# Loading the second chunk of two weight matrices in halves, and multiplying it half by half for two batches together

## The chip, the cores and the metric

The kernel runs on one core of one Trainium2 chip. The core has a matmul engine (PE, with its weight loads shown apart as PEld), a vector engine (DVE), an activation engine (ACT), a general engine (POOL) and a queue engine (SP), and 16 DMA engines that move data between the chip's main memory (DRAM) and the on-chip memory. The metric is the device time of one execution in microseconds; smaller is better.

## What is computed

The inputs are q, k and v of 8 batches x 8 heads x 576 positions x 64, a memory score phi of 8 x 8 x 576 x 32, and three weight matrices: gate and value (512 x 1536) and out (1536 x 512). Cut to what matters:

```python
a = softmax(phi, over the 576 positions)
k_m = einsum('bhsm,bhsd->bhmd', a, k)        # 32 memory slots per head
v_m = einsum('bhsm,bhsd->bhmd', a, v)
attn = softmax(scale * q @ k_m.T)            # 576 x 32 per head
x = attn @ v_m                               # (batch, 576, 512) over all heads
out = (silu(x @ w_gate) * (x @ w_val)) @ w_out
```

## The kernel before, in words

The kernel never forms x. For each batch it multiplies the small v_m (32 slots x 64 per head) by the gate and value weights first. The result is called U here: 8 heads x 32 slots = 256 rows by 1536 columns, once for gate and once for value. Then gate = attn @ U_gate and value = attn @ U_value. The 1536 columns are cut into three chunks of 512 (`CH`), and each chunk can be cut into two halves of 256 (`HC`).

**Loads of the weights.** `load_w(which, c, half)` (issue at L155) loads chunk `c` of the gate weights (`which` 0) or the value weights (`which` 1), from float32 in DRAM to bfloat16 on the chip. Without `half` it is one load of 512 KB with 512 columns in a row; with `half` it is one load of 256 KB with 256 columns in a row. The tile of a chunk in halves has the half as its outer dimension, and `w_part` (L158 to L164) picks the right slice for either layout. Before the change chunk 0 is loaded in halves (four loads of 256 KB) and chunks 1 and 2 whole (four loads of 512 KB).

**The POOL queue.** POOL issues all these loads, and also those of k, v, q, most of phi and the out weights, and it does arithmetic between them: in the opening it multiplies one attention tile (`norm(1, 1, nc.gpsimd)`, L512), and later it forms sums of activations (L637, L680). Its instructions run in the order written. The loads that POOL issues share eight semaphores in rotation, so that each load is issued only after the load eight places earlier has landed. The order of POOL's loads before is: k of batch 0, q of batch 0, k of batch 1, q of batch 1, v of batches 0 and 1, chunk 0 in four halves, chunk 1 (gate, value), chunk 2 (gate, value); then the multiplication L512; then out weights 0, k of batch 2, out weights 1, phi of batch 2, out weights 2, v of batch 2; then, between groups of sums, phi of batch 3, q of batch 2, q of batch 3, k and v of batch 3. In this text "q of batch 2" is the load issued at L125 at 42.64 us.

**The weight products.** `u_round` (L520 to L576) multiplies one or more parts of the weights by v_m of one batch. A part is one or two of gate and value, a chunk, and one or both halves. The 128 x 128 array of PE is used as eight tiles of 64 x 32, so eight matmuls (L531) run side by side. Each part fills two PSUM banks of 512 columns, which are then copied to the U tile by ACT (L560) and DVE (L564), in the order of the letters in `evac`. `u_item(b, c)` is one round with all of chunk c of gate and then of value: 16 matmuls of 512 columns and four copies of 512 columns. `u_half(b, (0, 1), c, half, evac)` is one round with one half of gate and of value side by side: 16 matmuls of 256 columns and two copies of 512 columns.

**The slots.** A slot (`gv_slot`, L622) is 128 of the 1536 columns for half the positions of one batch: two matmuls of 288 columns for the gate (p_g, L592), a silu on ACT (L609), and one slot later two matmuls for the value (p_v, L592) and a product on DVE (L615). A batch has 24 slots, eight to a chunk. `g0` and `g1` are the slots of batches 0 and 1. When the eight slots of a chunk are through, `chunk_done` (L663) hands sums over the chunk to POOL or DVE and issues some later loads.

**The order around the change.** Batches 0 and 1 run together. Everything is written out by hand (`manual_schedule`), so the order of the program is the order on each engine. Chunk 0 already runs in halves for both batches. Then, before the change, the loop over chunks 1 and 2 does: products of batch 0, some slots of batch 1's previous chunk, five slots of batch 0; products of batch 1, three slots of batch 0, five slots of batch 1. From batch 2 on, each batch needs its q transposed: `q_T` (L432 to L442) does that for batch 2 on PE with q as the loaded weights (p_q, L438), amid output products of batch 0 (L814) and the k and v sums of batch 2 (p_kv, L248).

Of the kernel before, what the change touches and what calls it, by code (L numbers as in the profile page):

```python
# [14 lines left out]
def kernel(  # L15
# [34 lines left out]
    NCH = DF // CH  # L50
# [46 lines left out]
    def load_k(b):  # L97
        t = inp.tile(
            [128, 2 * NP + (b % 2 == 0), JK * D], BF16, tag=f"kv{b % 2}", bufs=1, name="t_kv"
        )  # L100
        nc.gpsimd.dma_start(out=t[:, 0:NP], in_=head_pairs(k[b]))  # L101
        kvs[b] = t

    def load_v(b):
        t = kvs[b]
        if b in counted:
            out = t[:, NP + 1:2 * NP + 1][:, ::-1]
        else:
            out = t[:, NP:2 * NP]
        nc.gpsimd.dma_start(out=out, in_=head_pairs(v[b]))  # L110
# [32 lines left out]
    HC = CH // 2  # L143

    def load_w(which, c, half=None):

        src = (moe_w_gate, moe_w_val)[which]
        split = half is not None
        if not half:
            W[which, c] = wpool.tile(  # L150
                [128, 2, NP, HC] if split else [128, NP, CH], BF16,
                tag=f"W{which}{c}", name=f"W{which}{c}",
            )
        f0, n = (half * HC, HC) if split else (0, CH)
        nc.gpsimd.dma_start(  # L155
            out=W[which, c][:, half] if split else W[which, c],
            in_=src[:, c * CH + f0:c * CH + f0 + n].rearrange("(i p) f -> p i f", p=128),
        )  # L158

    def w_part(which, c, i, g, halves):  # L160

        w = W[which, c][64 * g:64 * g + 64]
        h0, h1 = halves[0], halves[-1] + 1
        return w[:, h0:h1, i] if c == 0 else w[:, i, HC * h0:HC * h1]  # L164

    WO, WOc, Ts = {}, {}, {}

    def load_wo(c):
        t = wpool.tile([128, 4, DM], BF16, tag=f"WO{c}", name=f"WO{c}")
        nc.gpsimd.dma_start(  # L170
            out=t,
            in_=moe_w_out[c * CH:(c + 1) * CH, :].rearrange("(i p) f -> p i f", p=128),
        )
        for i in range(4):
            WO[4 * c + i] = t[:, i]
        WOc[c] = t
# [333 lines left out]
    def norm(b, g, eng=nc.vector):  # L510
        a = att.tile([128, 2, HALF], BF16, tag=f"A{g}", name="t_A")
        eng.tensor_tensor(out=a, in0=es.pop((b, g)), in1=lzs.pop((b, g)), op=ALU.mult)  # L512
        atts[b, g] = a
# [6 lines left out]
    def u_round(b, parts, evac, later=None, sums=None):  # L520
# [3 lines left out]
        for which, c, halves in parts:  # L524
# [4 lines left out]
            def one(w, i, g, p=p, n=n, w0=w0, c=c, halves=halves):  # L529
                o = (w - w0) * n  # L530
                nc.tensor.matmul(  # L531
                    p[g][32 * i:32 * i + 32, o:o + n],
                    lhsT=kTs[b][64 * g:64 * g + 64, 2, 32 * i:32 * i + 32],
                    rhs=w_part(w, c, i, g, halves),
                    start=True,
                    stop=True,
                    tile_position=(64 * g, 32 * i),
                )
# [43 lines left out]
    def flush_mul(n=None):  # L582
        for _ in range(len(pend) if n is None else n):
            pend.pop(0)()
# [349 lines left out]
    def u_item(b, c, evac="avav"):  # L934

        return lambda: u_round(b, (((0,), c, (0, 1)), ((1,), c, (0, 1))), evac)

    def u_half(b, which, c, half, evac):

        return lambda: u_round(b, ((which, c, (half,)),), evac)  # L940
# [18 lines left out]
    def run(items):  # L959
        for x in items:  # L960
            x()
# [13 lines left out]
    def gv_slots(b):  # L975
        return [lambda s=s: gv_slot(b, s) for s in range(2 * NJF)]
# [36 lines left out]
    load_q(1)  # L1013
    load_v(0)
    load_v(1)
    for half in range(2):
        for which in range(2):
            load_w(which, 0, half)
    for c in range(1, NCH):
        for which in range(2):  # L1020
            load_w(which, c)
    for c in range(NCH):
        u_buffer(1, c, f"S{c}")

# [25 lines left out]
    z_inv(1, 1)  # L1050
    norm(1, 0)
    norm(1, 1, nc.gpsimd)
    load_wo(0)
    load_k(2)
    nc.gpsimd.memset(kvs[2][:, NP], 1.0)
# [9 lines left out]
    g0, g1 = gv_slots(0), gv_slots(1)  # L1065
# [15 lines left out]
    run(last_copy)  # L1081
    flush_mul(1)
    run(g1[2:4] + g0[4:8] + g1[4:6])
    for c in range(1, NCH):
        s = 8 * c
        run([u_item(0, c)] + g1[s - (2 if c == 1 else 3):s] + g0[s:s + 5])
        run([u_item(1, c)] + g0[s + 5:s + 8] + g1[s:s + 5])
    run(g1[-3:])
    flush_mul()
    backlog = []  # L1090

# [158 lines left out]
```

## Time and profile before

| | |
|---|---|
| median of 3 runs | 231.17 us (231.09 to 231.43) |
| profiled execution, its own time | 231.35 us |
| span of that execution | 229.6 us |
| PE busy | 221.1 us (96%) |
| DVE busy | 186.6 us (81%) |
| ACT busy | 171.2 us (75%) |
| POOL busy | 151.8 us (66%) |
| mean share of DMA queue q0 (POOL's loads) | 52.9% |

The span runs from the first to the last instruction; the device time has some 1.75 us around it. Times inside the profile are counted from the start of the span. A busy PE is not PE at its peak, since matmuls are pipelined, so the stretch around the change is read from the timeline and the chain of waits and not from the busy share. In a line of the timeline the columns are: start, length, engine, line of the program, operation, what is written and read with its shape, and how many instructions are merged; in brackets stands how long the engine had been idle and for what.

### The profile page before, as it was taken

To read this page: it belongs to the slowest core of one execution; us is meant where nothing else is said; L and a number is where in the kernel's file an instruction comes from. 1 tells how busy PE (TensorE), PEld (TensorE's weight loads), DVE (VectorE), ACT (ScalarE), POOL (GpSimd) and SP (SyncE) were. 2 spreads that over 40 slices of the span, in tenths; PEclk is the share of its full clock that TensorE was granted. 3 is DMA by queue.
4 is the path that set the end of the run, shared out by engine and by line. 5 is a ranking of instruction groups with operands and counts; after the bars stand their busy time and mean duration, and the time that the engine had idled before them with its cause. 6 is when DMAs were issued, how large, how long until landed. Compare 5 with 4: busy or idle time off the path is not lost.

```text
span 229.6 us, 7220 instructions
## 1 busy us (share of the span) xinstructions
PE 221.1 (96%) x2826; PEld 171.3 (75%) x2826; DVE 186.6 (81%) x425; ACT 171.2 (75%) x365; POOL 151.8 (66%) x207
## 2 busy tenths in 40 slices
PE   6986899999999999999999999999999999999993
PEld 2553576778887877888788887888788878878893
DVE  4156799999977999998997768998999899977832
ACT  2867988988446899988885758978898889677311
POOL 8422736999099759979986789467545764029291
PEclk9999999999999999999999999999999999999998
DMA  6999999999995998998199945995013502202024
GB/s 207 213 211 205 198 207 207 211 256 267 207 175 135 236 276 168 223 201 205 62 227 197 204 149 120 252 226 100 32 62 113 107 0 96 91 0 94 23 92 163
DMA packets 36546, 36.84 MB, mean 160 GB/s; under 512 B 14496, under 2 KB 30880, under 8 KB 36512
## 3 DMA queue, kind: packets, MB, share of 16 engines
q0 software_dynamic: 16272, 22.42, 52.9%
q1 hardware_dynamic: 19568, 13.24, 21.6%
q10 hardware_dynamic: 672, 0.72, 0.9%
q8 instruction: 22, 0.36, 0.6%
q14 instruction: 12, 0.10, 0.1%
HBM read 42.47 MB, written 9.44 MB: 226 GB/s over the span
## 4 chain that ended last, share of the span: by engine, by line
PE 87%; DMA 9%; POOL 2%; issue 0%; ACT 0%; POOLq 0%; ACTq 0%
PE p_g L592 21%; PE p_v L592 21%; PE p_os L814 20%; PE p_oc L814 10%; DMA W<-in_moe_w_val_dram 9%; PE p_oa L814 5%; PE p_u L531 5%; PE p_kv L248 2%; PE p_os L802 1%; PE p_g L451 1%; POOL t_kv L101 1%; POOL t_kv L110 1%; POOL t_q L125 0%; PE p_q L438 0%; POOL W L155 0%
## 5 line engine op out<-in xcount | busy, mean ns | idle before, releaser
L615 DVE TENSOR_TENSOR t_h<-t_sg,p_v 128x288 bf16<-128x288 bf16 x192 | 82.1, 451 | 12.5 <-PE p_v L592 6.6
L592 PEld LDWEIGHTS <-t_U 128*128 128x128 bf16 x768 | 74.0, 98 | 20.2 <-issue 2.7
L609 ACT ACTIVATE t_sg<-p_g 128x288 bf16<-128x288 f32 x192 | 74.3, 420 | 17.8 <-PE p_g L592 11.1
L592 PE MATMUL p_g<-t_A,t_U 128*128 128x288 bf16 x384 | 77.0, 286 | 0.0
L592 PE MATMUL p_v<-t_A,t_U 128*128 128x288 bf16 x384 | 77.0, 286 | 0.0
L814 PEld LDWEIGHTS <-t_S 128*128 128x128 bf16 x384 | 37.3, 98 | 4.6 <-issue 0.2
L680 POOL TENSOR_TENSOR t_S<-t_h 128x512 bf16<-128x512 bf16 x17 | 19.6, 1154 | 21.0 <-DVE t_h L615 19.7
L814 PEld LDWEIGHTS <-t_h 128*128 128x128 bf16 x288 | 27.0, 98 | 7.3 <-issue 3.5
L558 ACT CAST t_U<-p_u 128x512 bf16<-128x512 f32 x50 | 26.4, 608 | 4.8 <-PE p_u L531 4.8
L814 PE MATMUL p_os<-t_T,t_S 128*128 128x256 bf16 x192 | 23.7, 273 | 0.0
L637 POOL TENSOR_TENSOR t_S<-t_S,t_h 128x512 bf16<-128x512 bf16 x17 | 19.6, 1155 | 1.3
L637 POOL TENSOR_TENSOR t_S<-t_h 128x512 bf16<-128x512 bf16 x16 | 18.4, 1152 | 0.0
L637 POOL TENSOR_TENSOR t_S<-t_h,t_S 128x512 bf16<-128x512 bf16 x16 | 18.4, 1151 | 0.0
L531 PE MATMUL p_u<-W,t_kT 64*32 64x512 bf16 (+1 forms) x416 | 16.8, 363 | 0.5 <-DMA W<-in_moe_w_val_dram 0.4
L562 DVE CAST t_U<-p_u 128x512 bf16<-128x512 f32 x22 | 14.3, 684 | 1.5 <-PE p_u L531 1.4
L986 PE MATMUL p_warm<-bones 128*128 128x512 bf16 x44 | 13.2, 439 | 1.7 <-DVE bones L1008 1.7
L814 PE MATMUL p_os<-t_T,t_h 128*128 128x256 bf16 x96 | 14.8, 274 | 0.0
L392 ACT COPY t_q<-p_os 128x512 f32<-128x512 f32 (+2 forms) x12 | 5.5, 469 | 9.2 <-PE p_os L802 5.1
L814 PE MATMUL p_oc<-t_T,t_S 128*128 128x256 bf16 x96 | 12.1, 273 | 0.0
L814 PE MATMUL p_oa<-WO,t_h 128*128 128x256 bf16 x96 | 11.8, 273 | 0.0
L814 PE MATMUL p_oc<-WO,t_S 128*128 128x256 bf16 x96 | 11.8, 273 | 0.0
L814 PE MATMUL p_os<-WO,t_h 128*128 128x256 bf16 x96 | 11.8, 273 | 0.0
(115 smaller groups left out, 329.6 us busy)
## 6 DMA issues: line engine op xcount, KB each, us to landing
out_dram<-t_o SPq DMA_DIRECT2D x11, 512.0 KB, 3.1
t_kv<-in_k_dram POOLq DMA_DIRECT2D x8, 576.0 KB, 10.6
t_q<-in_q_dram POOLq DMA_DIRECT2D x8, 576.0 KB, 8.3
t_kv<-in_v_dram POOLq DMA_DIRECT2D x8, 576.0 KB, 15.6
t_phi<-in_phi_dram POOLq DMA_DIRECT2D x6, 576.0 KB, 8.2
out_dram<-t_o SPq DMA_DIRECT2D x10, 256.0 KB, 8.0
WO<-in_moe_w_out_dram POOLq DMA_DIRECT2D x3, 512.0 KB, 19.0
W<-in_moe_w_gate_dram POOLq DMA_DIRECT2D x2, 512.0 KB, 16.1
```

The lines of the kernel that those rows point to most:

```text
L248: nc.tensor.matmul(p[g][32 * i:32 * i + 32, 0:n], lhsT=phi_of(b, g, j, i), rhs=kv_of(b, slice(64 * g, 64 * g + 64), w0, w1, i, j), start=( ...
L392: nc.scalar.copy(out=out, in_=in_)
L531: nc.tensor.matmul(p[g][32 * i:32 * i + 32, o:o + n], lhsT=kTs[b][64 * g:64 * g + 64, 2, 32 * i:32 * i + 32], rhs=w_part(w, c, i, g, halve ...
L558: nc.scalar.copy(out=t, in_=p)
L562: nc.vector.tensor_copy(out=t, in_=p)
L592: nc.tensor.matmul(p[:, 0:HALF], lhsT=Us[b, c, g][:, o // 2, which, 128 * (o % 2):128 * (o % 2 + 1)], rhs=atts[b, g][:, r], start=(g == 0) ...
L609: nc.scalar.activation(out=sg, in_=gate[:, 0:HALF], func=AF.Silu)
L615: nc.vector.tensor_tensor(out=dst, in0=sg, in1=val[:, 0:HALF], op=ALU.mult)
L637: eng.tensor_tensor(out=out, in0=x, in1=y, op=ALU.subtract)
L680: eng.tensor_tensor(out=t[:, 0], in0=A21, in1=A22, op=ALU.add)
L814: nc.tensor.matmul(mine[home][:, u], lhsT=lhs(c, m, u), rhs=rhs(c, m), start=fresh and u == 0, stop=(k == 5), skip_group_check=u == 1 or n ...
L986: nc.tensor.matmul(p[:, 0:128 * a], lhsT=bones, rhs=x.to_broadcast([128, a, 128]) if a > 1 else bones, start=True, stop=True,)
```

## The change

The second chunk of the gate and value weights (c = 1) is loaded in four halves of 256 KB, in the order gate half 0, value half 0, gate half 1, value half 1, in place of two loads of 512 KB. The two loads of chunk 2 are issued later in POOL's program: behind the multiplication `norm(1, 1, nc.gpsimd)` and ahead of the out weights, so that still 14 loads stand ahead of that multiplication. The products of chunk 1 go by half chunks: half 0 for batch 0 and batch 1 one after the other, seven slots, half 1 for both, eight slots. The slots of the two batches are put in an order that fits: those of batch 0's chunk 1 come in two groups of four, and one slot of batch 1 follows each. Chunk 2 runs as before. In all later batches the matmuls with chunk 1 read the new layout of its tile.

```diff
@@ w_part
-        return w[:, h0:h1, i] if c == 0 else w[:, i, HC * h0:HC * h1]
+        return w[:, h0:h1, i] if c < 2 else w[:, i, HC * h0:HC * h1]
@@ the loads of the opening
-    for half in range(2):
-        for which in range(2):
-            load_w(which, 0, half)
-    for c in range(1, NCH):
-        for which in range(2):
-            load_w(which, c)
+    for c in range(2):
+        for half in range(2):
+            for which in range(2):
+                load_w(which, c, half)
@@ behind the attention of batch 1
     norm(1, 1, nc.gpsimd)
+    for which in range(2):
+        load_w(which, 2)
     load_wo(0)
     load_k(2)
@@ the slots of batches 0 and 1
     run(g1[2:4] + g0[4:8] + g1[4:6])
-    for c in range(1, NCH):
-        s = 8 * c
-        run([u_item(0, c)] + g1[s - (2 if c == 1 else 3):s] + g0[s:s + 5])
-        run([u_item(1, c)] + g0[s + 5:s + 8] + g1[s:s + 5])
-    run(g1[-3:])
+    for half, slots in enumerate((g1[6:8] + g0[8:12] + g1[8:9], g1[9:12] + g0[12:16] + g1[12:13])):
+        run([u_half(b, (0, 1), 1, half, "av") for b in range(2)] + slots)
+    run([u_item(0, 2)] + g1[13:16] + g0[16:21])
+    run([u_item(1, 2)] + g0[21:] + g1[16:])
     flush_mul()
```

## The prediction

> **What bounds the kernel now.** I read first the page's busy shares and the shares of the chain that ended last, then that chain in order of time, and then the timelines of PE and POOL where the change lies.
>
> ```profile
> PE 221.1 (96%) x2826; PEld 171.3 (75%) x2826; DVE 186.6 (81%) x425; ACT 171.2 (75%) x365; POOL 151.8 (66%) x207
> ...
> PE 87%; DMA 9%; POOL 2%; issue 0%; ACT 0%; POOLq 0%; ACTq 0%
> ```
>
> PE carries the end, after an opening that belongs to the DMA. The chain, in order of time (start, length, what):
>
> ```profile
> 6.74 20.12 DMA W<-in_moe_w_val_dram
> ...
> 34.71 0.56 PE p_u L531 x16
> ...
> 38.80 0.56 PE p_u L531 x16
> ```
>
> The value half 0 of chunk 0 lands at 6.74 + 20.12 = 26.86 us, last of the eight loads that PE needs to begin. Behind it the chain holds nothing but PE until the end of the kernel. PE's table of waits from 27 us to the end holds only the 0.4 us that this load ends, so a gain must come out of PE's own work and a loss must be a new PE wait. PE's timeline around a round in halves (chunk 0, today) and a whole round (chunk 1, today):
>
> ```profile
> 29.47 0.41 PE L592 MATMUL p_v<-t_A,t_U 128*128 128x288 bf16 x2
> 29.80 0.63 PE L531 MATMUL p_u<-W,t_kT 64*32 64x256 bf16 x32
> 30.37 0.66 PE L592 MATMUL p_v<-t_A,t_U 128*128 128x288 bf16 x4
> ...
> 34.30 0.41 PE L592 MATMUL p_v<-t_A,t_U 128*128 128x288 bf16 x2
> 34.64 0.62 PE L531 MATMUL p_u<-W,t_kT 64*32 64x512 bf16 x16
> 35.20 0.42 PE L592 MATMUL p_g<-t_A,t_U 128*128 128x288 bf16 x2
> ```
>
> From the last pair of a slot to the first of the next slot it is 30.37 - 29.47 = 0.90 us with 32 matmuls of 256 columns, and 35.20 - 34.30 = 0.90 us with 16 of 512.
>
> POOL's timeline shows when loads land, since each load waits for the one eight places earlier:
>
> ```profile
> 24.49 0.74 POOL L155 DMA_DIRECT2D W<-in_moe_w_val_dram  x1 [2.09 <-DMA t_kv<-in_v_dram]
> 25.27 1.29 POOL L512 TENSOR_TENSOR t_A<-t_E,t_lz 128x576 bf16<-128x576 bf16 x1
> 26.50 0.80 POOL L170 DMA_DIRECT2D WO<-in_moe_w_out_dram  x1
> ...
> 29.83 0.75 POOL L94 DMA_DIRECT2D t_phi<-in_phi_dram  x1 [0.43 <-DMA W<-in_moe_w_val_dram]
> 32.34 0.74 POOL L170 DMA_DIRECT2D WO<-in_moe_w_out_dram  x1 [1.76 <-DMA W<-in_moe_w_gate_dram]
> 34.90 0.74 POOL L110 DMA_DIRECT2D t_kv<-in_v_dram  x1 [1.81 <-DVE t_h L615]
> ```
>
> At 24.49 us v of batch 1 has landed, at 29.83 the four halves of chunk 0 behind it, at 34.90 the two whole loads of chunk 1 (the last line names DVE, but its load is the one eight behind the value weights of chunk 1). The stage table over those stretches (POOL busy, clock, DMA share, GB/s):
>
> ```profile
> 24.49:29.83 5.34, 4.77 (x6) 1.00 1.38 199
> 29.83:34.90 5.07, 1.49 (x2) 1.00 1.24 207
> ```
>
> The same megabyte takes 5.34 us in four halves and 5.07 us in two wholes. Last, the load of q of batch 2 and its user:
>
> ```profile
> 42.64 0.55 POOL L125 DMA_DIRECT2D t_q<-in_q_dram  x1
> ```
> ```profile
> DMA to landing us min/median/max: 16.7/16.7/16.7
> ```
> ```profile
> 58.99 0.61 PE L814 MATMUL p_oc<-t_T,t_S 128*128 128x256 bf16 x4
> 59.35 0.75 PEld L438 LDWEIGHTS <-t_q 128*128 128x128 bf16 x12
> 59.44 0.83 PE L438 MATMUL p_q<-ident,t_q 128*128 128x128 bf16 x12
> ```
>
> This load lands at 42.64 + 16.7 = 59.3 us and PE loads it as weights at 59.35. It comes just in time. It lies in one unbroken stream of loads: the DMA share is over 1 in every stretch of 2 us from 18 to 66 us.
>
> **The change part by part.**
>
> *Products of chunk 1.* Removed: two whole rounds at 34.64 and 38.73 us. Added: two pairs of half rounds, each 32 matmuls of 256 columns and 32 weight loads. By the rows above a pair costs 0.90 us against 0.90 us, so 0.00 us; I keep 0.02 as an upper bound, since the rows round to 0.01. The slots are the same in number: 7 + 8 before, 7 + 8 after, and the order from batch 1's slot 13 on is the old one.
>
> *Copies to U.* Four per round, two on ACT and two on DVE, before and after, of 512 columns each: 1.26 us for two on ACT and 1.40 us for two on DVE (35.11 and 35.19 us today). The first use comes two slots, 0.98 us, after the round, as now. DVE ends its second copy near 36.6 us, and PE wants that bank for the fourth pair after it, at 35.20 + 0.98 + 0.74 = 36.92. The 0.3 us between are the cover; ACT's first copy can start 0.05 us later (it needs 0.52 us after 29.80 in halves, 0.47 after 34.64 whole). Cost zero.
>
> *Later reads of chunk 1.* From batch 2 on its 512 columns are read as two runs of 256, as chunk 0 is now. A round of 24 matmuls, 16 on chunk 0 and 8 on chunk 1, takes 0.77 us in the chain, 32 ns a matmul, against 0.56 / 16 = 35 ns for chunk 1 alone. Bound 0 on both sides.
>
> *chunk_done.* Batch 0's chunk 1 finishes four slots (4 x 0.49 = 2.0 us) later, near 43.5 us. Its sums wait on POOL for their turn at 48.76 us, 5 us of cover, and for batch 1's slot 15, which does not move. Loads of k and v of batch 3 stand behind those sums and keep their place.
>
> *POOL.* Two more issues at 0.74 us. Fourteen loads still precede the multiplication L512, which waits for ACT, so it stays at 25.27; gate and value of chunk 2, moved from 21.66 and 24.49, go out at 26.50 and 27.3. With the rotation the others slip: the out weights to about 28.5, k of batch 2 to 29.83, the rest one landing each, v of batch 2 to 34.90 + 0.27 = 35.17. POOL is free at 35.9, before its first sum at 36.93. Since two loads were added, each load from phi of batch 3 on waits for the same load as now. SP's queue keeps its instructions; its first transposed load there needs q of batch 3, 0.3 us later with cover, since PE's scores with that q (L451) begin at 91.6 us.
>
> *DMA.* This is the one term that I find. No load changes its turn by bytes, and the stream stays full, since up to eight loads are in flight (15 to 20 us from issue to landing). But chunk 1 takes four transfers for two. Price: the rows 5.34 against 5.07 us give +0.27 us, 0.135 per added transfer. Bounds: by rate, 207 against 199 GB/s, 5.07 x 0.04 = +0.20; by the dearest pair of halves (26.86 to a landing of 12.49 + 17.1 = 29.6, so 2.73 us) 2 x 2.73 - 5.07 = +0.39. I take 0.27, which holds all four. What it delays: chunk 1's halves have cover (half 0 of both would land near 32.2 for 34.64; half 1 near 34.9 for 38.73), chunk 2 lands at 24.49 + 15.3 + 0.27 = 40.1 for 43.31. Out weights 0, k, phi and v of batch 2 have more than a microsecond each (v: 34.90 + 19.5 = 54.4 for 58.12). But q of batch 2 lands at 59.57 for a weight load at 59.35, where landing and load are 0 to 0.05 us apart today. PE then waits 0.22 to 0.27 us at p_q. All of batch 2, and the rest of PE's chain, stand behind it, and nothing there takes the time back.
>
> [...]
>
> Sum: 0.01 (products) + 0.25 (q of batch 2) = +0.26 us. The profiled execution's 231.35 becomes 231.61. It lies 0.18 above the median of the runs, so on the median's scale 231.17 + 0.26 = 231.43. A difference under 0.2%, 0.46 us, is about what a measurement can't tell from none, so this counts as no change with a lean to slower.
>
> **Rivals.**
>
> (a) The delay is hidden: in executions without a profile the loads may be a little earlier against PE. The profiled one is 0.18 us over the median, which would fit an opening, up to 26.86, slowed that much; then q of batch 2 has about 0.2 us of slack and costs 0.05. Or halves cost no more than wholes. Time 231.17 + 0.01 to 0.06, about 231.2. For it: the zero slack is a coincidence. Against: PE's start and this landing hang on the same stream, so both move together.
>
> (b) Slower by over 0.2%: the added transfers cost more than chunk 0's rows tell. Place: the same wait at p_q. It decides from 0.46 / 2 = 0.23 us per added transfer; the dearest pair of halves gives 0.195. At twice my price, 0.27, PE waits 0.54 and the time is 231.17 + 0.55 = 231.7. For it: loads of k and v of batch 2 and of phi share the stream until 59 us and my price is from one stretch. Against: four halves in a row already gave it.
>
> (c) Faster by over 0.2%: today the value weights of chunk 1 land at 18.77 + 15.8 = 34.6 us for matmuls that begin at 34.64; in runs where PE waits there, the change frees it, since half 0 is there 2.4 us ahead. It would have to remove over 0.46 us: 230.6. Against: the profiled execution waits 0.0 there, and a stream that is late at 34.6 is late at 59.3 too, where the change adds.
>
> (d) The change does what it says to order and loads; that PE itself runs differently (a bank or U not ready) I count into (b)'s side.
>
> **How the numbers follow.** Forecast (+0.1 to +0.45, own range 231.25 to 231.6): 0.48. Rival (a): 0.21. Rival (b), with (d): 0.24. Rival (c): 0.07. So faster 0.07, within 0.2% 0.48 + 0.21 = 0.69, slower 0.24. The time is the forecast's, 231.43. The range takes in (a) with 0.1 us of scatter below (the runs reach 0.08 under their median), 231.1, and (b) at twice the price with the same above, 231.8.
>
> **What would show it.** Right: POOL's load of v of batch 2 released near 35.2 in place of 34.90; chunk 1's rounds at 34.64 and near 38.7 with 32 matmuls in 0.56 us; PE idle some 0.25 us before p_q near 59.6 by the load of q; everything later shifted by that. Wrong: no idle time at p_q (rival a), over 0.45 us (b), or any new idle time of PE between 34 and 54 us (copies or banks late).

## The result and the profile after

The changed kernel took 232.05 us in the median of 20 runs (231.27 to 232.71). In the same session the kernel before took 231.11 us in the median of 20 runs (231.0 to 231.6). The ratio is 1.0038, with a 95% interval of 1.0027 to 1.0049: slower by about 0.9 us. The runs of the changed kernel also lie in a band twice as wide, 1.4 us against 0.6 us.

The profiled execution took 232.71 us with a span of 230.9 us, the slowest of those runs, 0.66 us above their median. The sum below is made against the profiled execution of before (231.35 us), so it has +1.36 us to explain, more than the medians differ.

Page of the changed kernel: busy shares, the row of the instruction queue (transfers, MB, share of 16 engines' span), and shares of the chain that ended last.

```profile
PE 220.2 (95%) x2858; PEld 171.1 (74%) x2858; DVE 186.7 (81%) x425; ACT 171.4 (74%) x365; POOL 153.4 (66%) x209
...
q8 instruction: 22, 0.36, 0.6%
...
PE 83%; DMA 10%; POOL 3%; ACT 1%; issue 1%; DVE 1%; POOLq 0%; ACTq 0%
```

PE was busy for 0.9 us less than before and yet ended later, so it stood idle. It runs 2858 matmuls and 2858 weight loads, 32 of each more than before. Its table of waits from 27 us to the end (us in total, times, longest) has two rows:

```profile
PE p_os L814 <- POOL t_S L637: 1.1, 1, 1.1
PE p_u L531 <- DMA t_kT<-t_bkv: 0.2, 1, 0.2
```

Neither is where the change lies. Where each of them falls is seen when the same instruction is timed in both kernels. After minus before is -0.20 us from 26.7 to 110 us, since this execution's opening happened to end 0.20 us sooner (first value half landed at 26.66 us against 26.86). It is +0.11 from 110.6 us on, and +1.41 from 134.1 us on (1.36 at the end). So there are two losses, 0.31 us and 1.30 us, and both are more than 65 us behind the changed part. PE's timeline of the changed kernel at the larger one:

```profile
132.30 0.41 PE L592 MATMUL p_g<-t_A,t_U 128*128 128x288 bf16 x2
132.54 0.41 PE L592 MATMUL p_v<-t_A,t_U 128*128 128x288 bf16 x2
134.10 0.60 PE L814 MATMUL p_os<-t_T,t_Q 128*128 128x256 bf16 x4 [1.14 <-POOL t_S L637]
```

The same place before:

```profile
132.44 0.41 PE L592 MATMUL p_v<-t_A,t_U 128*128 128x288 bf16 x2
132.69 0.60 PE L814 MATMUL p_os<-t_T,t_Q 128*128 128x256 bf16 x4
```

The bracket names a sum on POOL, because that sum ended at 132.88 + 1.15 = 134.03 us, just before PE went on at 134.10. It can't be the cause. Before, the same sum ended at 132.78 + 1.15 = 133.93 us, and the same matmuls had begun at 132.69. The sum on POOL after, and then before:

```profile
132.88 1.15 POOL L637 TENSOR_TENSOR t_S<-t_S,t_h 128x512 bf16<-128x512 bf16 x1
```
```profile
132.78 1.15 POOL L637 TENSOR_TENSOR t_S<-t_S,t_h 128x512 bf16<-128x512 bf16 x1
```

Further kernels below show the same idle time as "issue", that is, with nothing in the profile that PE waits for. What was on the DMA engines at that moment is in the DMA table of the stretch 131.0 to 133.5 us, in slices of 62 ns (busy share of the 16 engines, GB/s, then the instruction queue). After:

```profile
DMA  9999999999999999009000000000100100101019
GB/s 279 299 287 283 295 287 303 537 279 266 279 266 274 274 258 37 16 16 12 0 0 0 0 0 0 0 4 8 8 8 8 12 8 8 12 8 12 8 25 304
...
q8 instruction: 1, 0.02, 3.0%
```

Before, over the same stretch:

```profile
DMA  9999999999999999999905899898586999799999
GB/s 303 283 295 279 303 287 283 295 295 287 283 303 287 283 295 291 295 279 291 329 20 164 250 299 295 229 262 262 164 312 230 393 360 426 295 360 393 360 344 393
...
q8 instruction: 1, 0.02, 3.0%
```

Up to 132 us both are full: that is the transposing load of q of batch 5. Then the engines of the changed kernel stand nearly empty until 133.4 us, and those of before do not; this comes back below. In both, one transfer of 0.02 MB of instructions falls into this stretch. In the records of the transfers it begins at 131.49 us and lasts 1.18 us after, and at 132.22 us for 1.18 us before. The page has 22 such transfers with 0.36 MB, so 16 KB each, counted on the same 16 engines as the data. PE has 5716 recorded instructions, which is 260 for each transfer; before, 5652 and the same 22 transfers give 257. From the start of the first transfer to that of the last, PE began about 250 for each, in both kernels. By these counts PE's program itself arrives in pieces, of some 250 to 260 recorded instructions, which is an estimate.

### The profile page after: what moved, and what is told of

It reads as the page before. It is cut to its first block, busy times and chain, and to the rows that moved or that the text cites. A ratio compares the mean times of both kernels' runs of the same rounds, so it can differ in the third digit from the quotient of the medians.

```text
span 230.9 us, 7286 instructions
## 1 busy us (share of the span) xinstructions
PE 220.2 (95%) x2858; PEld 171.1 (74%) x2858; DVE 186.7 (81%) x425; ACT 171.4 (74%) x365; POOL 153.4 (66%) x209
## 4 chain that ended last, share of the span: by engine, by line
PE 83%; DMA 10%; POOL 3%; ACT 1%; issue 1%; DVE 1%; POOLq 0%; ACTq 0%
PE p_g L592 19%; PE p_os L814 19%; PE p_v L592 19%; PE p_oc L814 10%; DMA W<-in_moe_w_val_dram 9%; PE p_oa L814 5%; PE p_u L531 5%; PE p_kv L248 2%; DMA t_kT<-t_bkv 2%; PE p_os L802 1%; PE p_g L451 1%; POOL t_kv L101 1%; POOL t_kv L110 1%; POOL t_S L680 1%; POOL t_S L637 1%
## 5 line engine op out<-in xcount | busy, mean ns | idle before, releaser
L592 PEld LDWEIGHTS <-t_U 128*128 128x128 bf16 x768 | 74.0, 98 | 19.8 <-issue 2.3
L592 PE MATMUL p_g<-t_A,t_U 128*128 128x288 bf16 x384 | 77.0, 286 | 0.0
L592 PE MATMUL p_v<-t_A,t_U 128*128 128x288 bf16 x384 | 77.0, 286 | 0.0
L814 PEld LDWEIGHTS <-t_S 128*128 128x128 bf16 x384 | 37.3, 98 | 4.6 <-issue 0.2
L814 PEld LDWEIGHTS <-t_h 128*128 128x128 bf16 x288 | 27.0, 98 | 7.4 <-issue 3.6
L814 PE MATMUL p_os<-t_T,t_S 128*128 128x256 bf16 x192 | 23.7, 273 | 0.0
L814 PE MATMUL p_os<-t_T,t_h 128*128 128x256 bf16 x96 | 14.8, 273 | 0.0
L986 PE MATMUL p_warm<-bones 128*128 128x512 bf16 x44 | 12.5, 422 | 1.7 <-DVE bones L1008 1.7
L814 PE MATMUL p_oc<-t_T,t_S 128*128 128x256 bf16 x96 | 12.1, 273 | 0.0
L814 PE MATMUL p_oa<-WO,t_h 128*128 128x256 bf16 x96 | 11.8, 273 | 0.0
L814 PE MATMUL p_oc<-WO,t_S 128*128 128x256 bf16 x96 | 11.8, 273 | 0.0
L814 PE MATMUL p_os<-WO,t_h 128*128 128x256 bf16 x96 | 11.8, 273 | 0.0
```

The costliest lines, as they stand in the source:

```text
L592: nc.tensor.matmul(p[:, 0:HALF], lhsT=Us[b, c, g][:, o // 2, which, 128 * (o % 2):128 * (o % 2 + 1)], rhs=atts[b, g][:, r], start=(g == 0) ...
L814: nc.tensor.matmul(mine[home][:, u], lhsT=lhs(c, m, u), rhs=rhs(c, m), start=fresh and u == 0, stop=(k == 5), skip_group_check=u == 1 or n ...
L986: nc.tensor.matmul(p[:, 0:128 * a], lhsT=bones, rhs=x.to_broadcast([128, a, 128]) if a > 1 else bones, start=True, stop=True,)
```

## The experiments

Three theories. A: the change adds 64 instructions to PE's program (32 matmuls, 32 weight loads). PE gets its program in such pieces (the expectations, and the count of seams below, take 256 instructions, which lies in the estimate; no run shows it closer), so every later seam between pieces falls 64 instructions earlier in the work, and one piece comes too late where the transposing load fills the DMA engines. B: the two added loads leave the stream of transfers in another state, which lasts to 110 and 134 us. C: the new order of slots and rounds does it.

All ratios are to the kernel before, with 95% intervals; "idle" is PE's idle time after 27 us in the profiled execution, as its table of waits has it.

**The two parts alone.** `loads_only` has the four half loads and the old order of products:

```diff
-    for half in range(2):
-        for which in range(2):
-            load_w(which, 0, half)
-    for c in range(1, NCH):
-        for which in range(2):
-            load_w(which, c)
+    for c in range(2):
+        for half in range(2):
+            for which in range(2):
+                load_w(which, c, half)
...
+    for which in range(2):
+        load_w(which, 2)
```

> Chunk 1 loaded in halves and chunk 2's loads moved, as in the changed kernel, but its products batch by batch as before. PE's program has its old length. Theory A: 231.1, within 0.2 us of before, no idle PE near 133 us. Theory B: slower by 0.5 to 1.3 us. Theory C: no change. By the prediction's term for the loads it would be 231.4, with PE idle 0.25 us near 59.6 us.

`products_only` has the old loads and the new order of products, with its 64 more PE instructions:

```diff
-    for c in range(1, NCH):
-        ...
+    for half, slots in enumerate((g1[6:8] + g0[8:12] + g1[8:9], g1[9:12] + g0[12:16] + g1[12:13])):
+        run([u_half(b, (0, 1), 1, half, "av") for b in range(2)] + slots)
+    ...
```

> Chunk 1 loaded whole as before, its products by half chunks of both batches as in the changed kernel (64 more instructions on PE). Theory A: slower by 0.5 to 1.3 us, PE idle near 133 us. Theory B: no change. Theory C: slower by 0.5 to 1.3 us, as in the changed kernel, and pad64 is not.

Measured: `loads_only` 231.27 us, 1.0007 (0.9998 to 1.0015), no idle time. `products_only` 231.74 us, 1.0033 (1.0019 to 1.0046), scattered from 231.32 to 232.84 us. PE of `products_only` in the timeline:

```profile
132.31 0.41 PE L592 MATMUL p_v<-t_A,t_U 128*128 128x288 bf16 x2
133.04 0.60 PE L814 MATMUL p_os<-t_T,t_Q 128*128 128x256 bf16 x4 [0.32 <-issue]
```

The loads carry at most a small part of the loss and the products most of it, so B falls. A small wait of `loads_only` hides inside a round, where no table shows it: its whole round of chunk 1 takes 0.84 us, against 0.62 before, because the value half 1 landed at 34.73 us, amid the round.

```profile
34.45 0.84 PE L531 MATMUL p_u<-W,t_kT 64*32 64x512 bf16 x16
```

The changed kernel needs only the halves 0 at this point, and its round takes 0.63 us. A and C remain.

**64 instructions and nothing else.** `pad64` is the kernel before with 32 more matmuls, and so 32 more weight loads, in the opening, among the `warm` matmuls that PE runs while it waits for the loads. The second argument cuts wide matmuls into narrow ones, so PE's work is the same and its program is 64 longer.

```diff
-    warm(104)
+    warm(104, 42)
```

> The kernel before, with 32 more matmuls in the opening: the first warm-up of 104 column blocks is cut into 58 matmuls in place of 26, so that PE's program grows by 64 instructions (32 weight loads, 32 matmuls), as in the changed kernel, and loads, products and order stay. Theory A (PE's program comes in pieces of 256 instructions over the same DMA engines; 64 more instructions move every later piece against the transfers, and one comes too late): slower by 0.5 to 1.3 us, with the wide scatter of the changed kernel, and PE idle 1 to 1.4 us near 133 us. Theory B (the two more loads leave the DMA stream in another state): 231.1, no change. Theory C (the order of slots and rounds itself): 231.1, no change.

Measured: 231.69 us, 1.0019 (1.0009 to 1.0029), 230.99 to 232.41 us. PE's timeline:

```profile
132.60 0.41 PE L592 MATMUL p_v<-t_A,t_U 128*128 128x288 bf16 x2
133.32 0.60 PE L814 MATMUL p_os<-t_T,t_Q 128*128 128x256 bf16 x4 [0.31 <-issue]
```

Nothing of the change is in this kernel, and PE stops before the same instruction as in the changed one, with the same wide scatter. The time lies in A's range; the idle time, 0.31 us, is shorter than the 1 to 1.4 us that A expected. C can't explain the stop, since the order is that of before.

**The same length by another way.** `after_joint` keeps the changed loads and the changed order, but puts the gate and value halves of chunk 1 side by side in one tile, so that one matmul of 512 columns does what two of 256 did. PE's program is then as long as before the change. `joint_pad64` adds the 64 instructions of `pad64` to it.

```diff
+                W["both"] = wpool.tile([128, 2, 2, NP, HC], BF16, tag="Wboth", name="Wboth")
+            W[which, c] = W["both"][:, :, which]
 ...
+                nc.tensor.matmul(
+                    p[g][32 * i:32 * i + 32, 0:2 * HC],
+                    lhsT=kTs[b][64 * g:64 * g + 64, 2, 32 * i:32 * i + 32],
+                    rhs=W["both"][64 * g:64 * g + 64, half, :, i],
+                    ...
```

> The changed kernel with the gate and value halves of chunk 1 side by side in one tile, so that one matmul of 512 columns (gate 256, value 256) does what two of 256 did. Loads, order of rounds and slots are those of the changed kernel, and the opening is untouched; PE's program has the length of before. Theory A: 231.1 to 231.35, scatter as before (under 0.6 us), PE not idle near 133 us. Theory C (order of slots and rounds): 231.7 to 232.2.

> after_joint with the first warm-up cut into 58 matmuls in place of 26: again 64 more instructions on PE. Theory A: slower again, 231.5 to 232.2, with the wide scatter, PE idle at its 3521st recorded matmul or weight load. Theory C: as after_joint.

Measured: `after_joint` 231.06 us, 0.9998 (0.999 to 1.0007), no idle time. `joint_pad64` 232.63 us, 1.0058 (1.0041 to 1.0075), from 231.16 to 233.53 us. PE of `after_joint` at the place in question:

```profile
132.13 0.41 PE L609 MATMUL p_v<-t_A,t_U 128*128 128x288 bf16 x2
132.37 0.60 PE L831 MATMUL p_os<-t_T,t_Q 128*128 128x256 bf16 x4
```

The length of the program decides: the changed loads and order at the old length cost nothing, and 64 instructions added in the opening cost more than the whole change did, and more than the 231.5 to 232.2 us that A expected. One gap stays: the profiled execution of `joint_pad64` was among its quick ones (231.24 us) and shows no stop at this place, so its loss is seen in its times only.

**The transfer that is in the way.** `after_plain_q5` is the changed kernel with the load of q of batch 5 as a plain copy in place of a transposing load; PE's program keeps the changed length. `before_plain_q5` does the same to the kernel before.

```diff
+        if b == 5:
+            nc.sync.dma_start(out=qTs[b].rearrange("p n x -> p (n x)"), in_=qs[b])
+            return
```

> The changed kernel, but q of batch 5 is moved to its tile by a plain copy of the same bytes in place of the transposing load (its content is then not transposed, so the output of batch 5 is left wrong). If the piece of PE's program is late because that load holds the DMA engines from 123 to 134 us, PE is not idle near 133 us although the program has its 64 more instructions, and the time is 231.1 to 231.5. If it is late for another reason, the idle time stays and the time is 231.6 to 232.2.

> The kernel before with the plain copy of q of batch 5 in place of the transposing load (the output of batch 5 is left wrong). The control to after_plain_q5: there is no idle time near 133 us to take away, so 231.0 to 231.2. If it comes out 0.4 us or more faster, the plain copy gains something of its own and after_plain_q5 shows nothing.

Measured: 231.28 us, 1.0005 (0.9996 to 1.0014), and 231.07 us, 0.9998 (0.9989 to 1.0007). In `after_plain_q5` the stop is gone:

```profile
132.51 0.41 PE L595 MATMUL p_v<-t_A,t_U 128*128 128x288 bf16 x2
132.76 0.60 PE L817 MATMUL p_os<-t_T,t_Q 128*128 128x256 bf16 x4
```

So without the transposing load the longer program costs almost nothing, and that load alone, with the old program, costs nothing. It takes both. In the records the piece of program comes at 129.34 us in place of 131.49, and in the control at 130.73 in place of 132.22: with the transposing load it begins 1.5 to 2.1 us later.

**Other lengths.** By A the loss should come and go with the place of the seam. `pad32` and `pad96` are the kernel before with 32 and 96 more instructions.

```diff
-    warm(104)
+    warm(104, 21)
```
```diff
-    warm(104)
+    warm(104, 64)
```

> The kernel before with 16 more matmuls in the first warm-up, 32 more instructions on PE. Theory A: the seam between two pieces is reached 32 instructions later in the program than with 64 more, near 134.5 us, when the piece has just landed: 231.1 to 231.5, PE idle at most 0.3 us, and no idle time at the output product at 132.7 us. Theory B and C: 231.1.

> The kernel before with 48 more matmuls in the first warm-up, 96 more instructions on PE. Theory A: the seam comes 32 instructions earlier in the program than with 64 more, near 130 us, while the transposing load of q still runs; PE idle there for 0.3 to 3 us, and the time 231.5 to 233. Theories B and C: 231.1.

Measured: `pad32` 231.07 us, 1.0000 (0.9991 to 1.0009), no idle time. `pad96` 231.59 us, 1.0017 (1.0008 to 1.0026), 231.41 to 231.66 us. The `pad96` expectation named the wrong place: at its seam, now at 131 us, PE does not wait. It loses at 110 us, at the other of the two places of the changed kernel, and its scatter is narrow:

```profile
110.80 0.41 PE L531 MATMUL p_u<-W,t_kT 64*32 64x512 bf16 x8 [0.49 <-DMA t_kT<-t_bkv]
```

**Lengths of the changed kernel.** `after_pad192` adds 192 instructions in the opening, so that with the 64 the program is 256 longer than before and, by A, the seams are back in their old places of the work. `after_less64` and `after_less32` take matmuls out of the opening, so that it is as long as before, or 32 longer. The diff of `after_pad192`, in which the second pair of lines comes at three places:

```diff
-    warm(104)
+    warm(104, 104)
...
-    warm(8)
+    warm(8, 8)
```

Of `after_less64`:

```diff
-    warm(104)
...
-    warm(8)
...
-    warm(4)
...
-    warm(8)
...
-    warm(12)
+    warm(8)
```

Of `after_less32`:

```diff
-    warm(104)
+    warm(40)
```

> The changed kernel with 96 more matmuls in the opening's warm-ups, of the same columns in all, so that PE's program is 64 + 192 = 256 instructions longer than before: the pieces fall again where they fall before. Theory A: back to 231.0 to 231.3, no idle PE near 133 us. Theories B and C: 232.0, as the changed kernel.

> The changed kernel with 32 of the 44 warm-up matmuls of the opening left out (the first 104 column blocks, 8, 4, 8 and 4 of 12), so that PE's program has the length of before. Theory A (a late piece of PE's program): back to 231.0 to 231.3, PE not idle at its 3521st matmul or weight load nor at the output product at 132.7 us, provided that the clock stays full. Theories B (loads) and C (order): 231.7 to 232.2.

> The changed kernel with 16 warm-up matmuls of 512 columns fewer in the first warm-up (40 column blocks for 104), so that PE's program is 32 instructions longer than before, as in pad32. Theory A: 231.0 to 231.4, no idle PE near 133 us, if the opening does not suffer from the shorter warm-up. Theory C: 231.7 to 232.2.

Measured: 231.57 us, 1.0023 (1.0008 to 1.0037); 232.18 us, 1.0043 (1.0031 to 1.0056); and 231.5 us, 1.0024 (1.0014 to 1.0034). In time, all three miss what A expected. In the profiled executions the stop at 133 us is gone in the first two, as A says, but these edits also change the opening, and that costs by itself: in `after_pad192` PE waits 1.0 us for the first value half (0.4 before), and in `after_less64` its second group of slots waits for ACT. As tests of the total time they are inconclusive. PE's waits of `after_pad192` and `after_less64`:

```profile
PE p_u L531 <- DMA W<-in_moe_w_val_dram: 1.0, 1, 1.0
PE p_u L531 <- DMA t_kT<-t_bkv: 0.2, 1, 0.2
```
```profile
PE p_g L592 <- ACT t_U L560: 0.4, 1, 0.4
```

`after_less32` told more than it was made for. Its opening is late by 0.3 us too, but it also stops further on:

```profile
134.55 0.41 PE L592 MATMUL p_g<-t_A,t_U 128*128 128x288 bf16 x2
135.42 0.41 PE L592 MATMUL p_v<-t_A,t_U 128*128 128x288 bf16 x2 [0.46 <-issue]
```

This is another matmul of another step (L592, not L814). Counted along PE's recorded instructions it is the same one: the stops of the changed kernel, `pad64`, `products_only` and `after_less32` all fall at the 3521st, give or take one. The stop belongs to a place in the program, not in the work. The records of the transfers then give the size. They show when the piece that comes last ahead of that place had landed, and when PE went on:

| kernel | piece landed | PE goes on | between |
|---|---|---|---|
| after | 132.67 | 134.10 | 1.43 |
| `pad64` | 132.02 | 133.32 | 1.30 |
| `products_only` | 131.73 | 133.04 | 1.31 |
| `after_less32` | 134.13 | 135.42 | 1.29 |
| before | 133.40 | 136.23, no stop | 2.83 |
| `after_joint` | 132.95 | 135.81, no stop | 2.86 |
| `pad32` | 131.99 | 134.16, no stop | 2.17 |
| `after_plain_q5` | 130.28 | 132.64, no stop | 2.36 |
| `joint_pad64` | 130.10 | 132.42, no stop | 2.32 |

Where PE stopped, it went on 1.3 to 1.4 us after the landing; where it didn't stop, it came to the place 2.2 us or more after the landing. By this account before had some 1.5 us of slack at this seam (2.83 less 1.3), which is an estimate. The change uses it up: 64 instructions sooner is 3.5 us sooner in the work (132.7 against 136.2), while the piece came only 0.7 us sooner (132.67 against 133.40). With the 1.30 us of the other three, PE would go on at 132.67 + 1.30 = 133.97 us; it went on at 134.10.

The other seams bear this out. Counted on and back from this one in steps of 256 recorded instructions, the 14 traces have 295 seams. The four stops have the four shortest times from landing to use, 1.29 to 1.43 us. Behind the opening the next shortest are 1.54 us in `pad96` and 1.57 us in `joint_pad64`, both near 82 us, and PE doesn't stop there.

Something else goes with the stop. In the four kernels that stop, and in none of the others at this seam, 17 to 22 DMA packets hang together: each is in flight for 1.3 to 1.5 us, where such a packet otherwise took 0.02. In the changed kernel they are packets of the transposing load, and they hang from 131.92 to 133.46 us, which is the empty stretch in the DMA table above. PE goes on 0.5 to 0.6 us after they end. `after_pad192` has such a hang too, from 133.69 to 135.3 us, beside the next piece. It does not stop, since PE comes to that piece's seam at 136.66 us, 2.2 us after the landing at 134.43. So a hang alone stops nothing, but how much of the 1.3 us belongs to the piece and how much to the hang was not separated.

On the pieces, `after_pad192`, 256 instructions longer than before, has 23 transfers, one more than before: 257 recorded instructions for each (5908 / 23), in the estimate of 250 to 260.

## Why the prediction was wrong

The forecast was 231.43 us, range 231.1 to 231.8, with 0.24 on slower. The time was 232.05 us.

- **Products of chunk 1: the step that failed.** As an estimate of the round it was right. The chain of the changed kernel has both pairs of half rounds, with 32 matmuls in the time that 16 took, and no idle time of PE from 34 to 54 us:

```profile
34.51 0.56 PE p_u L531 x32
...
38.60 0.56 PE p_u L531 x32
```

  But the 64 added instructions were priced only by the time of their round, "0.00 us". They also lengthen PE's program and move the seams behind them in the work: the place of the 3521st recorded instruction came 3.5 us sooner (132.7 us against 136.2). The price of that was 1.30 us in the profiled execution, some 95 us later. The row `q8 instruction` stood in the page of before with its 22 transfers, and wasn't used.

- **DMA: right in price, wrong in effect, a second step that failed.** Four halves for two wholes were priced at +0.27 us. The records give 5.34 us from the landing of the last half of chunk 0 (29.38) to the last half of chunk 1 (34.72), against 5.07 us: +0.27. POOL's timeline of the changed kernel shows the landings at the issues that they release; v of batch 2 goes out at 35.00 us, predicted 35.17, with 0.20 us of the opening's luck between:

```profile
32.30 0.76 POOL L94 DMA_DIRECT2D t_phi<-in_phi_dram  x1 [0.40 <-DMA W<-in_moe_w_val_dram]
33.94 0.74 POOL L170 DMA_DIRECT2D WO<-in_moe_w_out_dram  x1 [0.88 <-DMA W<-in_moe_w_gate_dram]
35.00 0.74 POOL L110 DMA_DIRECT2D t_kv<-in_v_dram  x1 [0.32 <-DMA W<-in_moe_w_val_dram]
```

  The wait at p_q, 0.25 of the forecast's 0.26 us, did not come: 0 was measured. q of batch 2 was issued at 42.44 us and landed 16.3 us later, at 58.7 (before: 59.3), ahead of its weight load:

```profile
59.14 0.54 PEld L438 LDWEIGHTS <-t_q 128*128 128x128 bf16 x8
```

  The step that failed here is "It comes just in time". The slack of 0.05 us between landing and weight load was that of one execution. In the five other traces with the old loads (`pad32`, `pad64`, `pad96`, `products_only`, `before_plain_q5`) q of batch 2 lands 0.44 to 0.63 us ahead of its weight load; in `pad32` it lands at 58.52 for 59.10. With the changed loads (the changed kernel, `loads_only`, `after_joint`, `joint_pad64` and `after_plain_q5`) it lands 0.04 to 0.45 us ahead, and no wait for it shows. So a delay of the predicted size fits into the usual slack. In `loads_only` v of batch 2 still landed 0.14 us later than before (54.58 against 54.44). Whether the stream gives that back before q lands can't be told, because q's landing differs by 0.8 us among kernels with the same loads (58.49 us in `pad96`, 59.30 before).

- **Copies, later reads, chunk_done, POOL: right.** PE's only waits behind 27 us are the two above, and neither is for a copy or a bank, nor, as shown above, for the sum that one of them names.

- **Rivals.** (a), hidden at p_q, described that place rightly but not the time. (b) had the sign for a reason that did not occur: p_q, or "a bank or U not ready". That the time rose, the way the forecast leaned, is luck for the same reason. The wait that (c) names occurs in `loads_only` (0.84 us for the round) and in `products_only` (0.76 us, with the value weights landing at 34.57), but not in the profiles of before (0.62) or of the changed kernel (0.63), and no gain in time is seen. No rival held a loss outside the stretch of the change.

- **What stays open.** The smaller loss, at 110 us, is a wait for the transposing load of k of batch 4, which landed at 109.56 us before, 109.61 in `pad32`, 109.89 in `products_only`, 110.33 in `loads_only`, 110.57 after, 110.62 in `pad64` and 110.75 in `pad96`, for matmuls that want it near 110.4. The load takes 3.7 to 3.8 us in all of these; what differs is its issue, at 105.85 us before and 106.86 after. It moves with the program's length, but `loads_only`, of the old length, moves it too; its cause was not separated. When a piece is asked for, and what takes the 1.3 us between its landing and PE's next instruction, no view shows. That the loss differs from run to run, 0.2 to 1.6 us above before in the changed kernel, fits a race between the piece and the transposing load, but single runs without a profile can't show it.

## What to carry to other kernels

Count the instructions that a change adds to an engine's program, and not only their time: on PE here, which hardly ever waits, a longer program moved a seam of its instruction supply 3.5 us in the work, and beside a transposing load that seam cost a wait of 1.30 us some 95 us behind the change. The signs were idle time marked "issue", or put down to work that the instruction does not need (compare with the kernel before), a transfer of the instruction queue just ahead of it, and runs that scatter more than before. Adding as many instructions where they cost no time tells such a loss from the work itself, and one wider matmul in place of two narrow ones took it away (232.05 to 231.06 us here), though no version tried beat the kernel before.

## What the runs showed of the hardware

- 64 more PE instructions in an opening that waits for loads anyway cost 0.19% (`pad64`) or 0.6% (`joint_pad64` against `after_joint`); 32 more cost nothing measurable (`pad32`, 1.0000, 0.9991 to 1.0009).
- A piece of PE's program, by the count of the 22 transfers, is one DMA packet of 16 KB, in flight for 0.9 to 1.6 us, once for 3.1 us beside the transposing load (`products_only`). Where PE stopped for it, it went on 1.3 to 1.4 us after the landing.
- The transposing load of q of batch 5 is in flight for 10.8 us after its issue at 123.3 us, and SP's queue is held by the issue for 7.4 us of them:

```profile
123.33 7.39 SPq L134 DMA_TRANSPOSE t_qT<-t_q  x1
```

- Loads in halves ran a little below loads of whole chunks. Two stretches of about a megabyte in halves, from the stage table of `loads_only` (busy times, clock, DMA share, GB/s), stand against 207 GB/s for the whole chunk of before:

```profile
24.30:29.70 5.40, 4.95 (x98) 3.16 (x105) 4.36 (x13) 5.11 (x12) 4.25 (x5) 1.00 1.45 195
29.70:35.02 5.32, 5.30 (x82) 3.76 (x81) 5.23 (x14) 4.51 (x12) 3.49 (x5) 1.00 1.39 200
```
